# Windowed attention with a gated projection behind it: the same 1256 tasks written down in another order

## The chip, the core and the metric

The kernel runs on one core of a Trainium2 chip. The metric is the time of one execution on the device in microseconds (us). The engines of the core run at the same time, each through its own list of instructions in the order in which the program wrote them: TensorE (PE in the profile; its weight loads are PEld) multiplies into PSUM, VectorE (DVE) and ScalarE (ACT) read PSUM and do everything elementwise, GpSimd (POOL) is nearly unused, and SyncE (SP) issues DMAs. An instruction that waits holds up all that is behind it on its engine.

## The reference

There are 8 batches, 8 heads, 512 local and 32 global positions, head size 64. Local queries see the 32 global keys and the local keys at most 32 positions away; global queries see all 544 keys. The heads are put side by side (544 rows of 512 for each batch, the global ones ahead) and go through a gated projection with a causal convolution of 5 taps:

```python
s_ll = np.where(np.abs(pos[:, None] - pos[None, :]) <= 32, scale * q_l @ k_l.T, -1e9)
out_l = softmax(concat([scale * q_l @ k_g.T, s_ll])) @ concat([v_g, v_l])
out_g = softmax(scale * q_g @ k_all.T) @ v_all
x = concat([out_g, out_l]) as (batch, 544 positions, 512)
gate = sigmoid(sum_k conv_w[k] * x shifted by 4 - k positions)
return (gate * (x @ w_val)) @ w_out
```

## The kernel before, in words

The work is cut into 1256 named tasks. Each is a small Python function that issues a few instructions. The string `ORDER` (from line 60) lists all of them by name; the last loop of the kernel walks through the list and calls each function, under a manual schedule, so the list fixes the order of the instructions on every engine. It was written by a program that plans from costs of the tasks; the program is not part of the kernel. A name may carry two marks. `:ACT`, `:DVE` or `:SP` says which engine does it (a copy, a norm, a store), and `@46` in which of the 8 PSUM banks its result lies (here banks 4 and 6; a task that takes two neighbouring banks names the first). The dictionary `BY` holds the engines, `HOME` the banks.

There are 32 units u (a batch's pair of heads, 4 to a batch) and 16 pairs of units w. The tasks, with the lines of the profile that their instructions have:
- `iq` loads the keys and queries of a unit (592 KB), `ig` its values for the global queries, `iv` the local values of a pair (640 KB), `wi0` to `wi7` the quarters of the two weight matrices. All go through SyncE's queue at line 247 (`transfer`), where also most stores are issued (line 629).
- `s` computes the scores of a unit (lines 385 and 391, 72 matmul records), `mx` takes the row maximum (lines 396 and 398), `exp` the exponentials with their sums in two halves (line 406), `den` and `rec` the reciprocal (411, 415), `norm` multiplies a half by it (421 on ScalarE, as four instructions, or 423 on VectorE, as one), `t` transposes 32x32 blocks (429), `av` multiplies by the values (440, 160 records a pair), `xc` copies the result out of PSUM, `halo` fetches the four positions ahead of it.
- `gs`, `gmax`, `gexp`, `gt`, `gtc`, `gav`, `gden`, `grec`, `gnorm`, `gx`, `gxc` do the same for the global queries of a batch (lines 314 to 367; `gs` 32 records, `gt` 5, `gav` 80).
- `tap` and `conv` are the five taps (230 or 232, and 494), `pc` the same as a product with diagonal matrices for the first two units (510), `sig` the sigmoid (517), `xh` and `xl` split x into two parts of less precision (236 or 238, and 489).
- `g1.b.e.t` is a step of x @ w_val for batch b, output block e, input block t: three products of 128x512 (531). `gv` multiplies by the gate (538), `gh` and `gl` split again, `g2.b.r.e` is a step of the second product (555), `ob` copies a row block of 256 KB out of PSUM, `st` stores it. `.g.` in place of a batch is the part for the global positions of all batches; it comes last, and its second row block is done in two halves (`g2.g.1.0`, `g2.g.1.1`).
- `w0` to `w7` turn the 64-bit weights into two 32-bit parts (lines 204 to 214, 236, 283); `z` multiplies zeros to keep TensorE busy.

Three things decide what a place in the list means. Tiles come from rings of 1 to 6 buffers (`RINGS`: 4 for `qk`, 2 for `v`, 4 for `vg`, 2 for `ob`), so a task waits until the last reader of its buffer is done. A PSUM bank must be read out before the next task whose home it is writes it. And a load is held back until the last matmul that the list has ahead of it is done:

```python
ins = nc.sync.dma_start(out, in_).ins
if last_pe:
    tc.add_manual_dep(ins, last_pe[0].name, after, reason="a load's place in the line")
```

Of the kernel before, what the change touches and what calls it, by code (L numbers as in the profile page):

```python
# [65 lines left out]
w1.high:ACT w1.low gden0 t2 pc1.1 mx7 exp4.1 w2.s0:DVE pc1.2 exp5.0 xh0:ACT w3.s1 grec0 w3.s2 exp5.1 pc1.3 w2.s1 exp7.0
pc1.4 conv1.3:ACT w3.s3 wi4 den5 w2.s2 gnorm0 av1@24 ig5 exp7.1 wi7 pc0.0@0 ig7 den4 w3.s4 rec4 w2.s3 wi5 xc3:ACT iv2
rec5 ig6 norm4.1:ACT xc2:ACT gx0@1 den7 gs1@46 w2.s4 s6@2 norm4.0:ACT gxc0:DVE xh1:ACT tap3:ACT pc0.1 xl0 gmax1 iq8
tap2:ACT t4 gexp1.1 norm5.1:ACT xl1 halo1:ACT mx6 iq9 conv3.0 w2.high:DVE pc0.2 pc0.3 iq11 pc0.4 gexp1.0 fix1 g1.0.0.0@1
w3.high:ACT conv0.3:ACT exp6.0 g1.0.0.3 w3.low norm5.0:DVE g1.0.0.1 gt1.0@4 rec7 ig4 conv3.1 gt1.1@6 conv2.0 gtc1.0:ACT  # L70
g1.0.3.3@0 t5 iv3 exp6.1 conv2.1 iq10 fix0 s8@4 gtc1.1:ACT den6 g1.0.3.2 g1.0.0.2 gav1@6 g1.0.3.1 s9@2 norm7.0:ACT
w5.s0:ACT conv3.2 conv2.2 conv3.3 norm7.1:DVE sig0 gden1 conv2.3 w2.low g1.0.2.0@7 mx8 g1.0.2.1 sig1 g1.0.3.0 w5.s1
grec1 g1.0.2.2 w4.s0:ACT rec6 g1.0.2.3 mx9 gnorm1 gx1@6 exp8.0 gv.0.3 t7 gxc1:ACT w5.s2 exp8.1 exp9.0 g1.0.1.2@0
g1.0.1.3 w4.s1 g1.0.1.1 gv.0.2 w5.s3 g1.0.1.0 av2@46 gv.0.0 norm6.0:DVE norm6.1:ACT exp9.1 w4.s2 xc4:ACT gv.0.1 xc5:ACT
t6 ig10 gs2@02 iv5 w5.s4 w4.s3 w5.high:ACT gh.0.0:ACT ig11 gmax2 w5.low halo2:DVE den8 tap5:ACT ig9 gexp2.0 w4.s4 av3@46
iq12 ig8 gt2.0@0 gexp2.1 gt2.1@2 xc6:ACT gl.0.0 den9 s11@4 xc7:ACT w4.high:ACT s10@6 tap6:DVE gtc2.0:ACT w4.low
w6.s0:ACT w7.s0:ACT mx11 w6.s1 iv4 w6.s2 w7.s1 g2.0.0.0@0 g2.0.2.0@1 w7.s2 w6.s3 gtc2.1:ACT w7.s3 exp11.0 w7.s4 w6.s4
gh.0.1:ACT iq13 rec8 exp11.1 g2.0.1.0@2 g2.0.2.1 w6.high:DVE norm8.1:ACT w7.high:ACT g2.0.0.1 xh3:ACT g2.0.1.1
g2.0.3.0@3 iq14 gl.0.1 w6.low gav2@4 iq15 gden2 w7.low rec9 xl3 norm8.0:ACT g2.0.3.1 tap4:ACT g2.0.0.2 conv5.0 g2.0.0.3
t8 den11 g2.0.1.2 ob.0.0:ACT g2.0.3.2 g2.0.3.3 conv5.1 norm9.1:ACT halo3:DVE mx10 tap7:ACT g2.0.2.2 conv4.0 xh2:ACT  # L80
grec2 g2.0.2.3 ob.0.2:ACT g1.1.2.2@5 g2.0.1.3 xl2 g1.1.2.3 norm9.0:ACT gnorm2 exp10.0 s12@0 st.0.0:SP g1.1.1.0@4
st.0.2:SP ob.0.1:ACT t9 mx12 exp10.1 conv6.0 ob.0.3:ACT g1.1.2.0 g1.1.1.3 exp12.0 ig12 gx2@2 conv4.1 g1.1.1.1 conv6.1
rec11 den10 conv5.2 g1.1.3.2@3 st.0.3:SP gxc2:ACT conv7.0 g1.1.3.1 rec10 exp12.1 g1.1.0.0@2 conv6.2 conv5.3 conv4.2
g1.1.3.3 conv7.1 norm11.1:ACT av4@06 norm11.0:DVE g1.1.3.0 conv4.3 norm10.0:ACT g1.1.0.3 g1.1.2.1 norm10.1:ACT g1.1.0.1
g1.1.1.2 xc8:ACT conv7.2 st.0.1:SP t10 xc9:ACT conv7.3 g1.1.0.2 t11 conv6.3 halo4:ACT sig2 ig14 xh4:ACT gv.1.1 den12
gv.1.0 sig3 gv.1.2 av5@06 s13@4 gh.1.0:ACT xc10:ACT gv.1.3 gh.1.1:ACT gl.1.0 xc11:ACT gs3@02 rec12 mx13 gl.1.1
g2.1.2.0@6 g2.1.3.0@7 gmax3 tap8:ACT exp13.0 tap9:DVE conv8.0 xl4 g2.1.3.1 g2.1.2.1 iq16 ig15 exp13.1 g2.1.2.2 conv8.1
g2.1.3.2 g2.1.2.3 g2.1.3.3 xh5:ACT s14@4 gexp3.1 iq17 gexp3.0 xl5 ob.1.3:ACT s15@0 mx14 g2.1.1.0@7 st.1.3:SP tap10:ACT
g2.1.1.1 mx15 tap11:ACT ig13 halo5:DVE ob.1.2:ACT g2.1.1.2 exp14.0 g2.1.1.3 norm12.1:DVE exp14.1 den13 conv8.2 iv6
ob.1.1:ACT conv11.0 rec13 norm12.0:DVE conv10.0 g1.2.0.0@6 gt3.0@2 gt3.1@4 iq18 g1.2.1.1@7 g1.2.0.2 gtc3.0:ACT g1.2.0.3  # L90
gtc3.1:ACT gav3@4 g1.2.0.1 g1.2.1.3 g1.2.2.1@5 conv9.0 ig18 den14 norm13.1:ACT g1.2.1.0 t12 ig17 iv7 iq19 conv9.1
st.1.1:ACT exp15.0 conv8.3 conv10.1 conv9.2 gden3 norm13.0:ACT rec14 g1.2.2.3 t13 conv9.3 conv10.2 grec3 exp15.1
conv11.1 sig4 av6@02 norm14.0:ACT g1.2.1.2 den15 gnorm3 conv11.2 rec15 norm14.1:DVE g2.1.0.0@4 xc13:ACT g2.1.0.1 gv.2.0
st.1.2:SP conv10.3 xc12:ACT g1.2.2.0 gx3@6 tap12:ACT conv11.3 norm15.0:ACT gs4@02 gv.2.1 gxc3:ACT t14 s17@6 g2.1.0.2
gmax4 sig5 gexp4.1 mx17 gexp4.0 norm15.1:DVE g1.2.2.2 exp17.0 exp17.1 g2.1.0.3 tap13:DVE halo6:ACT g1.2.3.3@2 ig16 s16@0
ob.1.0:DVE g1.2.3.0 t15 xh6:DVE gt4.0@3 mx16 gh.2.0:DVE gtc4.0:ACT gv.2.2 gt4.1@6 gtc4.1:ACT den17 g1.2.3.2 g1.2.3.1
exp16.0 ig19 rec17 gv.2.3 conv12.0 gl.2.0 av7@36 exp16.1 s18@0 xc14:ACT iq20 s19@2 g2.2.0.0@4 g2.2.3.0@5 den16 xl6
g2.2.0.1 mx18 st.1.0:ACT gh.2.1:DVE norm17.0:ACT norm17.1:ACT iv8 xc15:ACT iq21 g2.2.3.1 exp18.0 gav4@6 rec16 gl.2.1
norm16.0:ACT t17 norm16.1:ACT iq22 exp18.1 g2.2.0.2 iq23 iv9 g2.2.1.0@7 ig23 halo7:DVE g2.2.0.3 conv12.1 xh7:DVE mx19
conv12.2 xl7 conv13.0 ob.2.0:ACT exp19.0 g2.2.3.2 s20@0 den18 g1.3.1.3@4 ig21 rec18 tap15:DVE gden4 exp19.1 norm18.1:ACT  # L100
# [5 lines left out]
g1.3.3.3@2 g1.3.3.1 g1.3.3.2 xh9:ACT halo9:DVE g1.3.2.1 g1.3.3.0 mx21 iq25 ig20 exp21.0 conv17.0 xl9 g1.3.2.3 tap19:DVE
gl.3.0 g1.3.2.0 exp21.1 gmax5 gexp5.0 st.2.2:SP gv.3.2 g2.3.0.0@0 gexp5.1 gv.3.3 conv19.0 g1.4.3.3@1 g1.4.3.0 gt5.0@2
gt5.1@4 g2.3.1.0@6 tap18:ACT g2.3.2.0@7 conv18.0 gtc5.0:ACT conv18.1 rec20 s22@2 gh.3.1:ACT gtc5.1:ACT den21 g2.3.2.1
conv19.1 rec21 conv18.2 gl.3.1 g1.4.3.1 mx22 norm21.1:ACT norm21.0:ACT norm20.1:ACT gav5@4 exp22.0 conv16.0 st.2.1:SP
t21 g2.3.0.1 g2.3.1.1 iv10 norm20.0:ACT conv19.2 g1.4.3.2 g2.3.2.2 conv17.1 gden5 g2.3.1.2 g2.3.0.2 grec5 g2.3.1.3 t20  # L110
exp22.1 den22 rec22 conv16.1 gnorm5 g2.3.2.3 g2.3.0.3 conv19.3 conv17.2 conv18.3 conv17.3 ob.3.1:ACT ob.3.2:ACT
norm22.0:ACT conv16.2 conv16.3 iq24 av10@24 sig8 sig9 gx5@7 st.3.1:SP g1.4.2.1@6 xc21:DVE g1.4.2.0 tap21:DVE ob.3.0:ACT
s23@4 gv.4.3 s24@0 mx23 xc20:ACT s25@2 gxc5:DVE g1.4.0.3@7 iq26 g1.4.0.1 g1.4.0.2 st.3.2:SP mx24 norm22.1:DVE mx25
tap20:ACT iv11 t22 g1.4.2.3 g1.4.2.2 g1.4.0.0 exp23.0 gv.4.0 exp23.1 exp25.0 exp24.0 exp24.1 den23 g1.4.1.2@4 halo10:DVE
rec23 iq27 g1.4.1.0 exp25.1 conv20.0 g2.3.3.0@7 g1.4.1.1 st.3.0:ACT g1.4.1.3 xh10:ACT norm23.0:DVE g2.3.3.1 g2.3.3.2
# [632 lines left out]
```

## Time and profile before

| what | us |
|---|---|
| runs of the kernel: median (lowest to highest) | 372.14 (370.38 to 375.02) |
| the profiled execution: its time | 370.21 |
| the profiled execution: span from first to last instruction | 368.4 |
| TensorE busy | 329.8 |
| VectorE busy | 310.5 |
| ScalarE busy | 266.9 |

The profile is of one execution. Between its span and its time lie 1.8 us that no instruction of the program shows. In a row of the timeline or of the waits, "issue" as the end of a wait means that the engine waited for no semaphore, queue or engine that the profile shows. A matmul's record is longer than the pitch at which matmuls follow each other, so a row of many is read by its whole length.

### The profile page before, as it was taken

Reading aid. Unit: us, or ns where it says so; the run is one execution under the profiler, and the core shown is the slowest. Engines: PE = TensorE matmul, PEld = TensorE weight load, DVE = VectorE, ACT = ScalarE, POOL = GpSimd, SP = SyncE. Lnnn points to the kernel's source line nnn. Section 1 sums busy time; section 2 is a strip of 40 time slices with the busy share of each in tenths; the row PEclk is TensorE's granted clock in tenths of the full one; section 3 lists DMA queues with packets and bytes.
Section 4 is the critical chain, followed back from the end, with each engine's and each line's share of the span. In section 5 each row is a group of like instructions: output and inputs, shape, how many; then the busy total and the mean of one; then the engine's idle time right before and its main releaser. Section 6 shows DMA issues by size and latency. Waiting matters only on the chain.

```text
span 368.4 us, 15320 instructions
## 1 busy us (share of the span) xinstructions
PE 329.8 (90%) x6736; PEld 257.4 (70%) x6736; DVE 310.5 (84%) x559; ACT 266.9 (72%) x855; POOL 1.0 (0%) x8
## 2 busy tenths in 40 slices
...
GB/s 284 377 389 74 132 357 240 2 282 147 189 95 40 97 234 252 63 104 200 369 12 4 161 87 100 264 121 269 169 73 202 75 69 91 30 2 30 86 59 114
DMA packets 19603, 54.76 MB, mean 149 GB/s; under 512 B 2128, under 2 KB 4560, under 8 KB 19536
## 3 DMA queue, kind: packets, MB, share of 16 engines
...
q8 instruction: 53, 0.87, 1.0%
...
## 4 chain that ended last, share of the span: by engine, by line
PE 63%; DMA 12%; DVE 12%; issue 6%; ACT 4%; SPq 1%; ACTq 0%; DVEq 0%
PE psum L531 19%; PE psum L555 18%; PE psum L440 9%; PE psum L385 8%; DMA qk<-in_qk_dram 5%; DVE gate L494 4%; DMA wraw<-in_w_val_dram 3%; PE psum L314 2%; PE psum L347 2%; DMA vg<-in_vgw_dram 2%; PE psum L331 2%; PE psum L510 2%; DMA craw<-in_convT_dram 1%; DVE pts L429 1%; DVE mx L396 1%
## 5 line engine op out<-in xcount | busy, mean ns | idle before, releaser
L406 ACT ACTIVATE pm<-psum,mx 128x128 f32<-128x128 f32 x256 | 90.5, 391 | 12.3 <-DVE mx L398 9.0
L494 DVE SCALAR_TENSOR_TENSOR gate<-xc,cw,gate 128x512 f32<-128x512 f32 x120 | 85.3, 741 | 0.6 <-ACT gate L230 0.2
L406 ACT ACTIVATION_READ_ACCUMULATOR pm<-psum,mx 128x1 f32 x256 | 59.1, 231 | 0.0
L385 PE MATMUL psum<-qk 64*32 64x128 f32 x2048 | 41.7, 279 | 16.7 <-issue 9.5
L531 PE MATMUL psum<-xh,wvh 128*128 128x512 f32 x128 | 53.4, 417 | 0.6 <-ACT pg L325 0.6
L396 DVE TENSOR_REDUCE mx<-psum 128x8 f32<-128x1024 f32 x32 | 38.9, 1217 | 16.6 <-PE psum L391 16.1
L555 PE MATMUL psum<-woh,gh 128*128 128x512 f32 x128 | 52.3, 409 | 0.0
L555 PE MATMUL psum<-wol,gh 128*128 128x512 f32 x128 | 50.5, 395 | 0.0
L555 PE MATMUL psum<-woh,gl 128*128 128x512 f32 x128 | 50.4, 394 | 0.0
L531 PE MATMUL psum<-xl,wvh 128*128 128x512 f32 x128 | 50.3, 393 | 0.0
L531 PE MATMUL psum<-xh,wvl 128*128 128x512 f32 x128 | 50.3, 393 | 0.0
L421 ACT ACTIVATE pm<-pm,mx 128x128 f32<-128x128 f32 x148 | 46.8, 408 | 4.8 <-DVE mx L415 4.6
L385 PEld LDWEIGHTS psum<-qk 64*32 64x32 f32 x2048 | 32.3, 107 | 25.4 <-issue 13.6
L440 PEld LDWEIGHTS psum<-pts,v 32*64 32x64 f32 x2560 | 38.1, 134 | 15.8 <-issue 9.1
L440 PE MATMUL psum<-pts,v 32*64 32x96 f32 (+3 forms) x2560 | 43.5, 264 | 6.0 <-issue 5.3
L429 DVE STREAM_TRANSPOSE pts<-pm 128x1024 f32<-128x1024 f32 x32 | 39.6, 1238 | 0.1
L531 PEld LDWEIGHTS psum<-xh,wvh 128*128 128x128 f32 x128 | 24.1, 188 | 8.5 <-issue 1.6
L555 PEld LDWEIGHTS psum<-woh,gh 128*128 128x128 f32 x128 | 24.3, 190 | 7.2 <-issue 2.1
L555 PEld LDWEIGHTS psum<-woh,gl 128*128 128x128 f32 x128 | 24.3, 190 | 5.4
L531 PEld LDWEIGHTS psum<-xh,wvl 128*128 128x128 f32 x128 | 24.0, 188 | 5.6
L517 ACT ACTIVATE gate<-gate 128x1024 f32<-128x1024 f32 x16 | 16.8, 1058 | 14.8 <-DVE gate L494 14.8
L555 PEld LDWEIGHTS psum<-wol,gh 128*128 128x128 f32 x128 | 24.4, 190 | 4.4
(106 smaller groups left out, 478.2 us busy)
## 6 DMA issues: line engine op xcount, KB each, us to landing
...
```

Of the source, the lines that this page charges most:

```text
L314: on_pe(T.matmul(s[h][SG * c:SG * c + SG, part], qkt[rows, C * GQ:C * GQ + C], qkt[rows, at:at + GH], start=True, stop=True))
L331: on_pe(T.transpose(pt[:, a, :], pg[:, h, P * a:P * a + P], ident))
L385: on_pe(T.matmul(s[h][C * j:C * j + C, P * i:P * i + P], qkt[rows, C * m:C * m + C], keys, start=(i == 0), stop=False))
L396: V.tensor_reduce(out=mx[:, :8], in_=banks(f"s{u}", 2).rearrange("p h (i c) -> p (h i) c", i=R), axis=AX.X, op=ALU.max, negate=True)
L406: A.activation(out=pm[:, h, i, :], in_=st[u]["s"][h][:, P * i:P * i + P], func=AF.Exp, bias=mx[:, c:c + 1], scale=SCALE, accum_out=mx[:, 8 ...
L421: A.activation(out=p[:, i, :], in_=p[:, i, :], func=AF.Copy, scale=rec[:, i:i + 1])
L429: V.transpose(out=st[w, "pts"][:, :, R * k:R * k + R].rearrange("p h i a q -> p h (i a q)"), in_=st.pop(u)["pm"].rearrange("p h i c -> p h ...
L440: on_pe(T.matmul(x[j // 2][D * h:D * h + D, j % 2, C * first:C * (first + count)], vt[rows, slot, h, :], p, start=(slot == 0), stop=stop))
L494: V.scalar_tensor_tensor(out=acc, in0=st[w, "xc"][:, t, k:k + SL], scalar=cw[:, u % NDT, k:k + 1], in1=acc, op0=ALU.mult, op1=ALU.add)
L517: A.activation(out=g, in_=g, func=AF.Sigmoid)
L531: on_pe(T.matmul(bank(f"g1.{key}.{e}")[:, :n], w[:, e, t * P:t * P + P], x, start=(d == 1 and q == 0), stop=(d == NDT and q == 2)))
L555: on_pe(T.matmul(o, g, w, start=(first and q == 0), stop=(last and q == 2)))
```

## The change

Only the text of `ORDER` differs: 1256 names before and after, the same names, in another order. The functions, rings, buffers and constants are the same, and each task issues the same instructions, except where a mark changes:
- engines: `norm` on ScalarE 41 of 64 halves (before 37), `halo` 11 of 15 (4), `ob` on ScalarE 32 of 35 (27, counting the two halves of the last block), `tap` 18 of 30 (20), `gtc` 16 of 16 (15), `gxc` 6 of 8 (5), `xh` 12 of 16 (13), the weights' first steps 2 of 8 (4) and their first copies 7 of 8 (6); the rest of each on VectorE. 28 of the 32 marked stores through SyncE (21) and 4 through ScalarE (11).
- banks: most `@` marks.

The diff, cut to the beginning, a piece of the middle and the end:

```diff
-iq0 iq1 iq2 iq3 wi0 iv0 wi1 iv1 wi2 wi3 cw z6.0@0 s0@0 gs0@24 dg0 mx0 gmax0 s1@6 dg1 exp0.0 exp0.1 w0.s0:DVE iq4 iq5
-s3@0 mx1 w0.s1 den0 gexp0.0 w1.s0:DVE exp1.0 rec0 w0.s2 gexp0.1 s2@2 gt0.0@4 exp1.1 z6.1@6 mx3 norm0.0:ACT ig0 w1.s1
-exp3.0 norm0.1:DVE mx2 iq6 iq7 den1 ig1 ig3 w1.s2 gtc0.0:ACT rec1 t0 exp3.1 norm1.1:DVE w0.s3 gt0.1@6 exp2.0 s4@4
-gtc0.1:ACT norm1.0:DVE w1.s3 ig2 w0.s4 t1 w0.high:ACT den3 exp2.1 mx4 av0@06 rec3 w0.low s5@2 norm3.1:DVE norm3.0:ACT
...
-g2.2.1.3 xh8:ACT gv.3.1 conv14.1 g1.3.0.2 den20 st.2.0:SP conv14.2 conv15.3 ob.2.1:ACT conv14.3 av9@04 tap16:ACT
-xc19:ACT halo8:ACT xc18:ACT st.2.3:SP gv.3.0 tap17:ACT xl8 gh.3.0:DVE g1.3.2.2@7 sig7 g2.2.2.3 s21@0 gs5@35 ob.2.2:DVE
...
-gv.g.1 g2.7.2.2 g2.7.1.3 ob.7.1:DVE gh.g.0:ACT g2.7.0.2 gv.g.3 g2.7.0.3 g2.7.2.3 gl.g.0 g2.g.1.0.0@5 g2.g.0.0@2
-ob.7.0:ACT gv.g.2 st.7.1:SP g2.g.0.1 gh.g.1:ACT gl.g.1 ob.7.2:DVE g2.g.1.0.2 g2.g.0.2 st.7.0:SP st.7.2:ACT ob.g.1.0:DVE
-g2.g.0.3 g2.g.1.1.0@3 ob.g.0:DVE g2.g.1.1.2 st.g.1.0 st.g.0 ob.g.1.1:ACT st.g.1.1
+iq0 iq1 iq2 iq3 wi0 iv0 wi1 iv1 wi2 wi3 cw z6.0@0 s1@0 mx1 dg0 s0@2 dg1 exp1.0 mx0 s3@4 mx3 z6.1@6 w0.s0:DVE exp1.1 den1
+gs0@06 w0.s1 rec1 w0.s2 gmax0 norm1.1:DVE ig2 iq4 exp0.0 exp3.0 exp0.1 w0.s3 iq5 norm1.0:ACT s2@2 den0 w1.s0:DVE gexp0.0
+gt0.0@0 rec0 w0.s4 w0.high:ACT norm0.1:ACT t1 w0.low gtc0.0:ACT gexp0.1 ig3 exp3.1 norm0.0:DVE w1.s1 mx2 t0 gt0.1@0
+w1.s2 w2.s0:DVE exp2.0 gtc0.1:ACT den3 w2.s1 rec3 w2.s2 w1.s3 w2.s3 norm3.1:DVE av0@46 exp2.1 den2 ig0 ig1 wi5 w2.s4
+norm3.0:ACT xc0:ACT s5@0 w1.s4 xc1:ACT rec2 halo0 pc0.0@6 pc0.1 w2.high:ACT w1.high:ACT mx5 s4@2 w1.low iq7 norm2.1:ACT
...
+sig1 s8@0 norm7.0:ACT xc5:ACT gh.0.0:ACT gav1@4 t6 ig11 w4.low iq11 mx8 g1.0.3.2 gl.0.0 g1.0.2.1 exp8.0 gden1 w7.s0:DVE
+grec1 exp8.1 ig8 w7.s1 s9@2 gv.0.3 gnorm1 norm7.1:ACT mx9 ig9 gv.0.2 gs2@04 tap5:ACT gmax2 g2.0.3.0@6 t7 w6.s1 exp9.0
...
+exp20.1 t18 gv.3.3 g1.3.2.0@2 mx21 g1.3.2.1 den20 halo8:ACT exp21.0 tap17:DVE g2.2.2.3 exp21.1 gh.3.0:DVE av9@63 gl.3.0
+tap16:DVE g1.3.2.2 g1.3.2.3 xc19:ACT gs5@03 xc18:ACT rec20 conv16.0 norm20.1:DVE den21 gv.3.2 gmax5 iv10 xh8:ACT
...
+g2.g.0.0@7 ob.7.1:DVE g2.g.1.0.0@6 gh.g.1:ACT g2.g.0.1 st.7.1:ACT gl.g.1 g2.g.1.0.2 ob.g.1.0:ACT g2.g.0.2 st.g.1.0
+g2.g.0.3 g2.g.1.1.0@6 g2.g.1.1.2 ob.g.0:ACT st.g.0 ob.g.1.1:ACT st.g.1.1
```

## Rows read from the trace of the kernel before

**Rows 1.** The page: its parts on engines (busy us, instructions) and on DMA queues

```profile
PE 329.8 (90%) x6736; PEld 257.4 (70%) x6736; DVE 310.5 (84%) x559; ACT 266.9 (72%) x855; POOL 1.0 (0%) x8
...
q8 instruction: 53, 0.87, 1.0%
```

**Rows 2.** Waits of TensorE, 0 to 100 us: waiting, ended by, total us, times, longest

```profile
PE psum L385 <- DMA qk<-in_qk_dram: 5.1, 5, 2.3
PE psum L385 <- issue: 4.8, 3, 2.8
PE psum L347 <- issue: 2.1, 2, 1.1
PE psum L314 <- issue: 1.3, 1, 1.3
PE psum L314 <- DMA qk<-in_qk_dram: 0.8, 1, 0.8
```

**Rows 3.** Waits of TensorE, 100 us to the end

```profile
PE psum L440 <- issue: 5.3, 6, 1.4
PE psum L385 <- issue: 4.8, 3, 2.3
PE psum L347 <- DMA vg<-in_vgw_dram: 2.5, 1, 2.5
PE psum L314 <- issue: 2.4, 2, 1.3
PE psum L385 <- DMA qk<-in_qk_dram: 1.4, 1, 1.4
PE psum L531 <- ACT pg L325: 0.6, 1, 0.6
```

**Rows 4.** Timeline of TensorE: start us, length us, line, what, count [idle before]

```profile
25.82 4.11 PE L440 MATMUL psum<-pts,v 32*64 32x256 f32 x160 [0.56 <-DVE mx L411]
...
31.40 0.74 PE L385 MATMUL psum<-qk 64*32 64x128 f32 x35 [0.89 <-issue]
...
34.81 1.22 PE L347 MATMUL psum<-vg,pgt 128*32 128x65 f32 x70 [1.13 <-issue]
...
40.45 2.44 PE L440 MATMUL psum<-pts,v 32*64 32x256 f32 x160
```

**Rows 5.** The chain that ended last, in order of time: start us, us, what

```profile
79.70 2.79 issue
...
92.33 5.68 PE psum L555 x24
...
208.80 1.09 PE psum L385 x64
...
243.61 2.28 issue
...
250.85 8.02 DMA vg<-in_vgw_dram
```

**Rows 6.** Windows: stretch, its us, busy us of each engine, clock, DMA share, GB/s

```profile
0.00:100.00 100.00, 83.53 (x2010) 60.36 (x2010) 81.87 (x169) 82.08 (x284) 1.04 (x8) 0.95 0.63 227
100.00:290.00 190.00, 172.96 (x3992) 136.40 (x3998) 166.94 (x283) 155.60 (x503) 0.00 (x0) 1.00 0.42 142
```

**Rows 7.** Instructions by line, ScalarE: busy us, mean ns | idle before, ended by

```profile
L421 ACT ACTIVATE pm<-pm,mx 128x128 f32<-128x128 f32 x148 | 46.8, 408 | 4.8 <-DVE mx L415 4.6
...
L236 ACT COPY ob<-psum 128x512 f32<-128x512 f32 x26 | 15.3, 589 | 16.3 <-PE psum L555 14.9 <-DMA out_dram<-ob 1.1
...
L517 ACT ACT_TABLE_LOAD x7 | 9.0, 1283 | 0.9 <-DVE gate L476 0.8
```

**Rows 8.** Timeline of VectorE, from 11 to 13 us

```profile
11.21 1.36 DVE L321 TENSOR_REDUCE gm<-psum 128x1 f32<-128x544 f32 x2 [1.52 <-PE psum L314]
...
12.68 0.42 DVE L206 TENSOR_SCALAR wa<-wraw 128x512 int32<-128x512 int32 x1
```

**Rows 9.** Timeline of ScalarE, the last copy

```profile
364.07 0.37 ACT L236 COPY obg<-psum 128x256 f32<-128x256 f32 x1 [5.03 <-DMA out_dram<-obg]
```

More of the change, by code (lines that the diff above doesn't have):

```diff
@@ L66 @@
[L66 to L100, printed above, removed]
@@ L106 @@
[L106 to L115, printed above, removed]
@@ L116 @@
-conv21.0 gv.4.2 g2.3.3.3 gv.4.1 ob.3.3:ACT gs6@02 norm23.1:DVE den24 t23 st.3.3:SP ig24 den25 gh.4.0:ACT gh.4.1:DVE iv12
-av11@46 gmax6 gexp6.0 gexp6.1 gl.4.1 xc22:ACT xc23:ACT gt6.0@0 gl.4.0 tap22:ACT gt6.1@2 s26@4 rec24 rec25 s27@6
-gtc6.0:DVE mx26 g2.4.3.0@0 norm25.0:DVE halo11:DVE iq29 iq30 norm25.1:ACT ig27 gtc6.1:ACT tap23:ACT g2.4.3.1 xh11:DVE
-g2.4.3.2 ig26 ig25 g2.4.2.0@1 xl10 exp26.0 xl11 g2.4.3.3 t25 g2.4.2.1 g2.4.1.0@2 conv21.1 conv20.1 conv21.2 norm24.0:ACT
-ob.4.3:ACT norm24.1:ACT mx27 st.4.3:ACT g1.5.3.3@0 exp26.1 g2.4.2.2 conv22.0 exp27.0 g2.4.1.1 g2.4.1.2 den26 conv20.2
@@ new lines @@
+exp16.0 conv10.2 exp16.1 t14 conv11.1 exp17.0 ig18 g1.2.2.1 g1.2.3.1 st.1.2:SP iq19 g1.2.3.0 ig19 exp17.1 g1.2.2.3
+g1.2.0.3 tap12:ACT conv10.3 g1.2.0.2 conv11.2 ig16 conv11.3 sig5 g2.1.0.3 av7@03 xc15:ACT xc14:ACT xh6:DVE g1.2.2.2
+g1.2.0.1 den16 xl6 gv.2.3 gv.2.2 gv.2.0 xh7:ACT g1.3.1.0@4 gs4@02 xl7 gmax4 tap15:ACT halo6:ACT s18@6 ob.1.0:ACT
+gh.2.0:ACT iv8 gexp4.1 mx18 iq21 iq20 rec16 st.1.0:SP gexp4.0 den17 ig17 g1.3.0.0@5 g1.3.1.1 gh.2.1:DVE gl.2.0 g1.3.1.2
+g1.3.1.3 g1.3.0.1 halo7:ACT gt4.0@0 g1.3.0.3 norm16.1:ACT gtc4.0:ACT gl.2.1 conv13.0 conv12.0 tap14:DVE g2.2.3.0@2
@@ new lines @@
+exp18.0 conv12.1 exp18.1 s19@0 g2.2.0.0@3 g2.2.0.1 norm16.0:ACT rec17 mx19 norm17.1:ACT conv13.1 iq23 den18 t16 gt4.1@6
+gtc4.1:ACT g2.2.0.2 g2.2.3.1 conv13.2 g2.2.3.2 conv12.2 norm17.0:ACT g2.2.3.3 exp19.0 ob.2.3:ACT t17 gav4@6 g2.2.0.3
+conv13.3 conv15.0 conv12.3 exp19.1 conv15.1 ob.2.0:ACT conv14.0 gden4 g2.2.1.0@7 rec18 sig6 g2.2.1.1 conv14.1 grec4
+den19 g1.3.0.2 g2.2.1.2 st.2.3:SP gnorm4 av8@02 ig20 norm18.1:ACT conv15.2 rec19 xc16:ACT iv9 xc17:ACT g1.3.3.1@6
+g2.2.1.3 g1.3.3.3 conv14.2 gx4@2 norm19.0:DVE ig22 ob.2.1:ACT s21@0 st.2.1:SP norm19.1:ACT gv.3.1 conv15.3 s20@3 gv.3.0
@@ new lines @@
+g2.2.2.0@5 conv14.3 mx20 gxc4:ACT iv11 g1.3.3.2 norm18.0:ACT t19 sig7 exp20.0 g2.2.2.1 iq22 st.2.0:SP g2.2.2.2 g1.3.3.0
+exp20.1 t18 gv.3.3 g1.3.2.0@2 mx21 g1.3.2.1 den20 halo8:ACT exp21.0 tap17:DVE g2.2.2.3 exp21.1 gh.3.0:DVE av9@63 gl.3.0
+tap16:DVE g1.3.2.2 g1.3.2.3 xc19:ACT gs5@03 xc18:ACT rec20 conv16.0 norm20.1:DVE den21 gv.3.2 gmax5 iv10 xh8:ACT
+gh.3.1:ACT s23@6 ob.2.2:ACT g2.3.3.0@2 g2.3.2.0@5 gl.3.1 st.2.2:SP g2.3.2.1 ig21 gexp5.1 iq26 mx23 rec21 gexp5.0 gt5.0@0
+g2.3.2.2 ig23 halo9:ACT conv16.1 norm20.0:ACT t20 tap19:DVE norm21.0:DVE g2.3.3.1 xh9:ACT iq25 g2.3.2.3 g2.3.3.2 s22@3
@@ new lines @@
+exp23.0 gtc5.0:ACT conv17.0 ob.3.2:ACT mx22 norm21.1:ACT g2.3.3.3 xl9 g2.3.0.0@5 conv17.1 exp23.1 gt5.1@0 gtc5.1:ACT
+iq24 g2.3.0.1 g2.3.0.2 ob.3.3:ACT t21 gav5@0 g2.3.0.3 exp22.0 st.3.2:SP conv17.2 st.3.3:SP xl8 conv16.2 iq27 den23
+exp22.1 g1.4.0.2@1 den22 g2.3.1.0@2 g1.4.0.1 av10@36 g2.3.1.1 gden5 rec22 tap18:ACT grec5 rec23 ob.3.0:ACT conv18.0
+g1.4.0.0 norm23.1:DVE gnorm5 conv17.3 norm23.0:ACT conv16.3 g2.3.1.2 conv19.0 norm22.1:DVE norm22.0:ACT xc20:ACT s24@3
+st.3.0:SP ig27 ig25 conv18.1 xc21:ACT t22 s25@5 mx24 g1.4.0.3 sig8 mx25 g1.4.1.2@7 g1.4.1.1 gv.4.0 t23 exp24.0 conv19.1
```

86 lines of the change are left out of this document (58 added, 28 removed).

## The prediction, made before the changed kernel ran

> **What bounds the kernel now.** I began with the page: TensorE is busy for 329.8 of 368.4 us, VectorE for 310.5, ScalarE for 266.9 [rows 1]. TensorE sets the time, and the first thing to read is why it ever stands still. Its waits, read once up to 100 us and once after, answer that. Up to 100 us 4.8 + 2.1 + 1.3 = 8.2 us are ended by "issue" (nothing that the profile shows) and 5.1 + 0.8 = 5.9 us by a load that landed [rows 2]; after it 5.3 + 4.8 + 2.4 = 12.5 us and 2.5 + 1.4 = 3.9 us [rows 3]. The largest wait on another engine after 100 us is 0.6 us. An order that has ScalarE or VectorE done earlier would gain little; one that removes part of the 20.7 and the 9.8 would.
>
> **What "issue" is.** Queue 8, kind instruction, moved 53 packets with 0.87 MB [rows 1], 16.4 KB each. TensorE has 6736 matmuls and as many weight loads, and 13472 / 53 = 254: one packet carries about 127 matmuls with their loads; I call that a line. In TensorE's timeline two stops follow each other at 31.40 and 34.81 us [rows 4], with 127 matmuls from one to the other (eight rows of S, mask and value products stand between). So a stop comes at the end of a line, and a line with little work still takes 34.81 - 31.40 = 3.4 us. The work in it is far less: 64 products of S take 1.09 us [rows 5], 160 of av 2.44 us [rows 4], so 128 of either are 2.0 to 2.2 us. 24 products of a projection take 5.68 us [rows 5]: a line of those lasts 30 us and never stops. A stop is then 3.4 us less the work of its line, and that work depends on which tasks the order puts side by side.
>
> [...]
>
> **Part 1, short lines.** I walked both orders, adding matmuls as the code issues them (s 72, av 160, gs 32, gav 80, gt 5, a g1 or g2 task 3), cut them every 127.6 through the stop at matmul 733 (34.81 us), and priced each line with the rows above. Before: 19 lines under 3.4 us, together 20.4 us short, against 20.7 measured; so I trust the sum (single lines agree less well: first rival). After: 13 lines, 9.4 us short. The change sets projection triples between the runs of av and s; only av0, av8, av11, av12 and av15 still hold a whole line. Lines 16 to 50 begin at about 100 us:
> - Lines 16 to 50: 12.4 us short before (12.5 measured), 6.0 after. TensorE is busy 173.0 of 190 us there, VectorE 166.9, ScalarE 155.6 [rows 6], so TensorE's time is the stretch's: **-6.4**.
> - Lines 1 to 15: 7.9 before, 3.4 after; this goes into part 3.
>
> **Part 2, loads after 100 us.** A load is issued when the TensorE task ahead of it in the order is done and its buffer is free, so its lead is the TensorE work between that place and its first reader. The 3.9 us stood at iq20 and iq21 (lead 4.7 to 8 us) and at ig25, ig26 (6.2 us; two qk and three vg loads were issued together, and one took 8.02 us [rows 5]). In the new order the shortest leads here are 6.5 (ig24, ig26), 6.6 (ig23), 7.1 (ig14) and 7.5 us (iq22). I leave 0.6 us for them: **-3.3**, between 0 (a crowded load takes 8.0 again) and -3.9. Seven more stores go through SP (28, before 21), and a load behind a store waits for that store's copy. The loads of the shortest leads have at most one such store ahead, so I count 0; if that fails, it eats the 3.3.
>
> **Part 3, the head.** TensorE could gain 4.5 us from lines and some of the 5.9 from loads (iq4 and iq5 were awaited before s4; now av0 stands between them and their reader). But VectorE and ScalarE are busy 82 of these 100 us each [rows 6] and start late. The new order does max 1, 0 and 3, then w0.s0, which could run at 12.68 us [rows 8], and then gmax0. That needs gs0, which now stands behind s3 and behind the first line's stop: VectorE waits some 2.7 us there where it waited 1.52 [rows 8]. From then to t0, on which av0 waits, I count 9 us, so av0 starts near 25.5, as before (25.82), and probably again at the half clock that made it 4.11 instead of 2.44 us [rows 4]. By a quarter of TensorE's work VectorE has been given as much work as before (84 against 85 us) and ScalarE 1.5 us more. Of their 18 idle us, 8 lie before 16 us; of the other 10 perhaps half were waits on TensorE's stops and come back: 5, less 1.0 lost at the start: **-4.0**, with 0 and -8 as ends.
>
> **Part 4, work that changes engine.** Four norm halves go to ScalarE, 4 x 4 x 0.408 = 6.5 us; five result copies too, at about 0.59 (three of them shorter), 2.7 us [rows 7]; the small ones (halo, tap, gtc, gxc, weights) give -0.6. VectorE loses about 6 us. Sigmoid and exp alternate 19 times instead of 13, so six more table loads at 1.283: 7.7 us [rows 7]. ScalarE gets 16.3 us more. From 100 to 290 us it has 34 us idle, so most is covered; but part of that cover was there because TensorE stood still. With fewer stops a PSUM bank must be read sooner after it is written. One place I can see is gs2, which needs the bank that exp8.1 reads, behind a table load, while TensorE has some 3 us of work. I charge **+3.0**: no row shows such a wait, the nearest (0.6 us, on ScalarE [rows 3]) is small; the ends are 0 and 16.3.
>
> **Part 5, the end.** The last copy waits until 364.07 for the store of the first half [rows 9]; it does so again, after the same last products: 0.
>
> Sum: -6.4 - 3.3 - 4.0 + 3.0 = -10.7. The profiled execution took 370.2 (span 368.4 and 1.8 around it), so 359.5. It was a quick one, the median of the runs being 372.14, 1.9 more: 361.4. I say **361**.
>
> **Rivals.**
> 1. *The fetch is late, not only slow.* The stops from 79.70 and 243.61 us took 2.79 and 2.28 us [rows 5], where those lines held 2.9 us of work each and my bound gives 0.5. The new order lifts lines from 2 us to just above the floor: 12 of its lines hold 3.4 to 4.5 us, 5 of the old. If each of the 12 stops 0.5 us, the 6.4 shrinks to 0.4: 367. For it: the load queues are busy 42% of the middle stretch [rows 6]. Against it: the sum over all lines met the measured one. Chance 0.22.
> [...]
> 3. *ScalarE takes over.* All of its 16.3 us lands ahead of bank reads that TensorE awaits: 372.14 - 13.7 + 16.3 = 375, slower. It decides from 13.7 us of such waits on. For it: six table loads stand ahead of an exp, and exps free the banks of s. Against it: 0.6 us of such waits now. Chance 0.06.
> 4. *The head gives 8 and nothing is lost to ScalarE*: 372.14 - 17.7 = 354. Chance 0.10.
>
> **How the numbers follow.** Forecast 0.54, rivals 0.22, 0.08, 0.06, 0.10. Two per cent, about what a measurement of this kernel can tell from no change, is 7.4 us: faster is under 364.7, slower over 379.6. The forecast's own range is 357 to 365.5, a tenth of it over 364.7: faster 0.48 + 0.10 + 0.02 (of rival 1) = 0.60; slower, half of rival 3, 0.03; within, 0.37. The range takes in rival 1 and the better part of rival 4: 354 to 369.
>
> **What would show it.** Right: TensorE's waits on "issue" fall to 9 to 11 us and those on loads to 5, none over 2 after 100 us; stops remain in av8, av11, av12 and av15; ScalarE shows 19 table loads after the first and some 283 us busy. Rival 1: stops of 0.5 to 2 us in lines that hold 3.4 to 4.5 us. [...] Rival 3: TensorE's waits on ScalarE over 13. The head is wrong if av0 starts before 24 or after 28 us.

## The result, and the profile after

| | before | after |
|---|---|---|
| median of the runs, us (lowest to highest) | 371.46 (370.38 to 375.02) | 358.61 (357.83 to 361.46) |
| ratio, 95% interval | | 0.965 (0.957 to 0.974) |
| the profiled execution: its time, us | 370.21 | 357.83 |
| its span, us | 368.4 | 354.9 |

The changed kernel is faster. Run twice more beside other kernels it came to 0.954 (0.949 to 0.959) and 0.958 (0.956 to 0.961) of the kernel before, so a single comparison of it is good to about half a per cent. I forecast 361.0 us with a range of 354 to 369: the time is right. Of the steps under it, the first 100 us came out on the other side, and the part behind them gave half as much again as foreseen.

The page of the changed kernel, engines (busy us, share, instructions) and DMA queues, against [rows 1]:

```profile
PE 328.3 (93%) x6736; PEld 255.5 (72%) x6736; DVE 304.5 (86%) x545; ACT 278.6 (78%) x887; POOL 1.0 (0%) x8
...
q8 instruction: 52, 0.85, 1.0%
```

TensorE does the same work in 13.5 us less span, with one packet fewer on queue 8 (one such packet is what I call a fetch from here on). The waits of TensorE in the changed kernel, first from 0 to 100 us (waiting, ended by, total us, times, longest), against [rows 2]:

```profile
PE psum L331 <- ACT pg L325: 5.2, 2, 3.7
PE psum L391 <- issue: 3.3, 1, 3.3
PE psum L440 <- issue: 3.3, 1, 3.3
PE psum L347 <- issue: 1.8, 1, 1.8
PE psum L385 <- DMA qk<-in_qk_dram: 1.3, 2, 0.7
PE psum L314 <- ACT pm L406: 1.3, 2, 1.0
PE psum L385 <- ACT xc L236: 1.2, 1, 1.2
```

and from 100 us to the end, all of them, against [rows 3]:

```profile
PE psum L440 <- issue: 2.1, 2, 1.2
PE psum L331 <- ACT pg L325: 0.6, 1, 0.6
PE psum L331 <- ACT xc L236: 0.3, 1, 0.3
```

The second list carries the gain. After 100 us the stops on "issue" fall from 12.5 to 2.1 us and the waits on loads (2.5 + 1.4, and 0.3 of a second kind) from 4.2 to nothing: 14.6 us. Waits on ScalarE grow by 0.3. The first list shows none of it: "issue" 8.2 before and 8.4 now; loads fall from 5.9 to 1.3, and ScalarE takes their place, 8.2 us with the smaller rows, 0.9 before.

The windows of the changed kernel (stretch, its us, busy us of PE, PEld, DVE, ACT, POOL, clock, DMA share, GB/s), against [rows 6]:

```profile
0.00:100.00 100.00, 80.71 (x1927) 57.39 (x1928) 79.78 (x162) 81.75 (x295) 1.05 (x8) 0.91 0.61 211
100.00:290.00 190.00, 187.27 (x4290) 148.19 (x4289) 176.86 (x300) 171.67 (x556) 0.00 (x0) 1.00 0.48 157
```

From 100 to 290 us TensorE goes from 173.0 to 187.3 us busy out of 190. In the first 100 us it loses 2.8 busy us and the mean clock falls from 0.95 to 0.91. The two orders do different tasks there, so I priced the matmuls done by 100 us as the prediction does: 73.2 us of TensorE's own work before, 69.4 after (70.9 in a second execution). By this estimate the changed kernel is 2.3 to 3.8 us behind at 100 us.

### The profile page after: what moved, and what is told of

Same layout as the page of the kernel before. It is cut to its first block, busy times and chain, and to the rows that moved or that the text cites. A ratio compares the mean times of both kernels' runs of the same rounds, so it can differ in the third digit from the quotient of the medians.

```text
span 354.9 us, 15327 instructions
## 1 busy us (share of the span) xinstructions
PE 328.3 (93%) x6736; PEld 255.5 (72%) x6736; DVE 304.5 (86%) x545; ACT 278.6 (78%) x887; POOL 1.0 (0%) x8
## 4 chain that ended last, share of the span: by engine, by line
PE 72%; DVE 15%; ACT 5%; issue 4%; DMA 2%; SPq 0%; ACTq 0%; DVEq 0%
PE psum L555 23%; PE psum L531 22%; PE psum L440 10%; PE psum L385 7%; DVE gate L494 3%; PE psum L347 3%; DMA qk<-in_qk_dram 2%; DVE pts L429 2%; DVE mx L396 2%; PE psum L331 2%; PE psum L314 2%; PE psum L510 2%; DVE gm L321 1%; ACT pm L406 1%; DVE xl L489 1%
## 5 line engine op out<-in xcount | busy, mean ns | idle before, releaser
L406 ACT ACTIVATION_READ_ACCUMULATOR pm<-psum,mx 128x1 f32 x256 | 60.5, 236 | 0.0
L555 PE MATMUL psum<-woh,gh 128*128 128x512 f32 x128 | 53.3, 416 | 0.0
L421 ACT ACTIVATE pm<-pm,mx 128x128 f32<-128x128 f32 x164 | 52.4, 413 | 0.4 <-DVE mx L415 0.4
L440 PEld LDWEIGHTS psum<-pts,v 32*64 32x64 f32 x2560 | 38.0, 135 | 15.1 <-issue 8.2
L440 PE MATMUL psum<-pts,v 32*64 32x96 f32 (+3 forms) x2560 | 42.8, 266 | 6.5 <-issue 5.4
L385 PE MATMUL psum<-qk 64*32 64x128 f32 x2048 | 38.1, 278 | 2.5 <-DMA qk<-in_qk_dram 1.3
L385 PEld LDWEIGHTS psum<-qk 64*32 64x32 f32 x2048 | 31.1, 107 | 11.8 <-issue 6.1
L538 DVE TENSOR_TENSOR gv<-psum,gate 128x512 f32<-128x512 f32 x32 | 21.8, 685 | 7.8 <-PE psum L531 5.3
L236 ACT COPY ob<-psum 128x512 f32<-128x512 f32 x29 | 17.2, 601 | 14.2 <-PE psum L555 10.9
```

What stands on the lines that cost most here:

```text
L236: A.copy(out, in_)
L385: on_pe(T.matmul(s[h][C * j:C * j + C, P * i:P * i + P], qkt[rows, C * m:C * m + C], keys, start=(i == 0), stop=False))
L406: A.activation(out=pm[:, h, i, :], in_=st[u]["s"][h][:, P * i:P * i + P], func=AF.Exp, bias=mx[:, c:c + 1], scale=SCALE, accum_out=mx[:, 8 ...
L421: A.activation(out=p[:, i, :], in_=p[:, i, :], func=AF.Copy, scale=rec[:, i:i + 1])
L440: on_pe(T.matmul(x[j // 2][D * h:D * h + D, j % 2, C * first:C * (first + count)], vt[rows, slot, h, :], p, start=(slot == 0), stop=stop))
L538: V.tensor_tensor(out=box["gv", p][:, k], in0=bank(f"g1.{key}.{e}")[:, :n], in1=gates[w0 + p][:, k], op=ALU.mult)
```

## The experiments

**1. Do stops belong to lines?** Dummy products of 64 columns behind gt0.0 move every later line boundary against the tasks by 16 or by 64 matmuls; no task changes its place.

```diff
+            if name == "gt0.0":
+                for _ in range(16):        # 64 in the second kernel
+                    T.matmul(psum[:C, 1, 2 * P:2 * P + 2 * C], eye[:D], mask[:D, :2 * C], start=True, stop=True)
```

> The changed order with 16 small matmuls of constants put behind gt0.0, where TensorE has 3.7 us to wait; nothing of the result depends on them. They push every later line boundary back by 16 matmuls of the order's own, so other tasks share a line. Theory A (stops come at line boundaries, and the new order was fitted to where they lie): lines 19, 24, 32, 45 and 48 are now short without long products right before them, and stops after 100 us grow from 2.1 us to 6 to 9 us; the time grows by 3 to 6 us over the changed kernel (ratio to before 0.974 to 0.982). Theory B (stops belong to the small matmuls themselves): stops stay at 2 us and the time within 1 us (0.965). Theory C (3.4 us less the line's own work, as in the prediction, whatever comes before the line): 7.2 us of short lines against 6.0, so 1.2 us more.

> As the run before, with 64 of the small matmuls in place of 16: some 1 us of work in a gap of 3.7 us. It is the control for what the added matmuls cost themselves. Theory A: the boundaries fall again so that long products stand before every short line; stops after 100 us stay at 1 to 3 us, the time within 1.5 us of the changed kernel (ratio 0.962 to 0.970). Theory B: the same. If the added matmuls cost by themselves, this run is slower than the one with 16.

With 16: 363.15 us, 0.973 of before (0.967 to 0.978). With 64: 356.14, 0.955 (0.950 to 0.959), no slower than the changed kernel itself. The waits of TensorE after 100 us with 16 dummies (columns as above):

```profile
PE psum L440 <- issue: 5.3, 4, 1.6
PE psum L391 <- issue: 1.6, 1, 1.6
...
PE psum L531 <- issue: 0.3, 1, 0.3
```

7.2 us of stops where the changed kernel has 2.1, and 3.5 with 64 dummies. Sixteen tiny products cost 5 us or more (0.973 against the 0.954 and 0.958 of the changed kernel alone, measured at other times; 5.1 us of it are these stops) and 64 cost nothing: what counts is where the boundaries fall. Stops belong to lines.

**2. What hides a fetch?** In the changed kernel av8, av11, av12 and av15 each hold a whole line, done in 1.8 to 2.1 us, and show no stop where the prediction's bound asks for 1.4 each. Their boundaries stand 2, 4, 3 and 5 matmuls behind projection triples. The kernel before has the same kind of line with other distances (worked out from its trace: packets of queue 8, and TensorE's starts at the boundaries):

```
line's products   matmuls between the last    fetch begins, us from       stop at the
                  long products and boundary  TensorE's passing boundary  line's end, us
before av4        30                          +0.52                       1.40
before av10       22                          -0.15                       0.66
before av9        12 (9 long ones ahead)      +0.72                       1.16
before av13       14 (gs7 between)            +1.08                       1.27
before av15       10                          -0.31                       0.41
before av12       7                           -0.27                       none
after  av12       3                           -0.55                       none
after  av11       4                           -1.17                       none
after  av8        2                           -2.27                       none
after  av15       5                           -3.03                       none
```

So the fetch of the next line may begin before TensorE reaches the boundary. I read it so: TensorE's sequencer, whose waits for semaphores the profile records (PEldq), runs ahead while long products (0.23 us each) wait to be done. In the trace of before its wait in front of av4 is on record at 105.4 us, 1.7 us ahead of av4's first product. To test that on one line, six triples of the kernel before went from right behind av4 to right ahead of it, which leaves 12 matmuls of av4 ahead of the boundary in place of 30 and the 128 matmuls of the line what they were.

```diff
-av4@06 norm11.0:DVE g1.1.3.0 conv4.3 norm10.0:ACT g1.1.0.3 g1.1.2.1 norm10.1:ACT g1.1.0.1 g1.1.1.2 ... g1.1.0.2
+g1.1.3.0 g1.1.0.3 g1.1.2.1 g1.1.0.1 g1.1.1.2 g1.1.0.2 av4@06 norm11.0:DVE conv4.3 norm10.0:ACT norm10.1:ACT ...
```

> The order before, with six triples of the projection (g1.1.3.0, 0.3, 2.1, 0.1, 1.2, 0.2) moved from right behind av4 to right ahead of it. The line boundary in av4 stood 30 matmuls into it and stands 12 into it now; the 128 matmuls up to the next boundary are products of av4 as before, 1.95 us. Theory A (the sequencer runs ahead of TensorE while long products stand before a boundary, so that the fetch begins earlier): the stop at the end of that line, 1.4 us, falls to 0.6 or less. Theory B (the prediction's bound: 3.4 us less the line's work): it stays at 1.4. Both: the other stops unchanged within 0.3 us. The time changes by 1 us at most, too little to read by itself.

373.44 us, 1.001 (0.997 to 1.005). TensorE's timeline around av4 (start us, length us, line, what, count [idle before]), first before:

```profile
107.07 2.40 PE L440 MATMUL psum<-pts,v 32*64 32x256 f32 x157
110.87 0.33 PE L440 MATMUL psum<-pts,v 32*64 32x32 f32 x3 [1.40 <-issue]
```

then with the triples ahead:

```profile
110.69 0.39 PE L531 MATMUL psum<-xh,wvl 128*128 128x512 f32 x1
111.01 2.44 PE L440 MATMUL psum<-pts,v 32*64 32x256 f32 x160
114.10 2.13 PE L440 MATMUL psum<-pts,v 32*64 32x256 f32 x97 [0.66 <-ACT xc L236]
```

All 160 products of av4 run through. The fetch began 2.84 us before TensorE passed the boundary, not 0.52 after it (0.85 after it, with a stop of 1.47 us, in the trace of experiment 3, where av4 stands as before). Long products ahead of a boundary let the fetch begin early, and the fixed floor of the prediction falls. The time did not move: av5, which the triples no longer separate from av4, now waits 0.66 us for ScalarE, and the s behind it 1.8 us for VectorE. The other stops did not stay as they were, as I had expected: the next three (1.27, 0.44 and 1.12 us) are gone too, with waits on VectorE and on a load in the place of two of them, and the one near 246 us is 0.5 us shorter. All stops after 100 us add up to 8.5 us here, 12.5 before.

**3. Loads alone.** The kernel before with four loads moved up, all matmuls in place:

```diff
-s16@0 ... iq20 ... iq21 ... iq27 ... ig26 ig25
+s16@0 iq20 iq21 ... iq27 ig26 ig25 ...
```

> The order before, with four loads moved up alone: iq20 and iq21 right behind s16, ig25 and ig26 right behind iq27; nothing else differs and no matmul changes its place. Theory A (part 2: the waits on loads after 100 us are lost time of TensorE): the waits on loads after 100 us fall from 4 us to under 1 and the time by 3 to 4 us, to 0.990 of the kernel before. Theory B (the wait is only moved: what stands behind is late for another reason): waits on loads gone, the time within 1 us. Theory C (loads moved up stand in the way of the fetches): the stops on issue after 100 us grow, from 12.5 to 14 or more, and the time is the same. If late fetches come from loads in flight, the stop of 2.3 us at 246 us changes too, since two of the five loads around it are now elsewhere: to 1 or less.

371.39 us, 0.992 (0.988 to 0.997): about 2.9 us of 373. The waits of TensorE after 100 us:

```profile
PE psum L440 <- issue: 6.5, 6, 1.5
PE psum L385 <- issue: 4.5, 4, 1.9
PE psum L314 <- DMA qk<-in_qk_dram: 2.9, 1, 2.9
PE psum L314 <- issue: 1.8, 1, 1.8
```

The waits at iq20, iq21 and at ig25, ig26 are gone, and part of them came back as time. One of 2.9 us on a load that was not moved (for gs4) stands here; it was 0.3 in the trace of before and 2.6 in the experiment on av4, so it seems to vary between executions. Stops stayed at 12.8 us: loads moved up do not get in the way of fetches here. The stop of 2.3 us near 246 us measured 1.6, but 1.7 in the experiment on av4, where no load was moved, so that expectation has no support.

**4. The head.** Edits of the changed kernel: without the zeros z6.1 (below); with the loads iq7 and iq6 right behind gt0.1; both; and, in two versions, the beginning rewritten with gs0 ahead of s3 and without the zeros.

```diff
-s3@4 mx3 z6.1@6 w0.s0:DVE
+s3@4 mx3 w0.s0:DVE
```

> The changed order without z6.1, six products of zeros that stand between s3 and gs0 and whose result nobody reads (left out). In the profile of the changed kernel they take 2.9 us at the half clock, between the first stop and gs0, on the chain that leads to av0 at 28.97 us. Theory A (the head is a chain over gs0, gmax0, gexp0, and the zeros are on it): gs0 starts 2.9 us earlier, av0 1 to 2.9 us earlier, the whole 1 to 2.5 us less (ratio 0.958 to 0.963). [...]

> The changed order with the loads iq7 and iq6 (issued at 37.4 and 42.8 us) right behind gt0.1, at about 28 us, when few loads run. Theory A (a fetch that is asked for while loads run starts late: the one that ended the stop of 3.28 us at 48.85 started 5.0 us after its boundary was reached, 1.1 us being the usual): the stops at 41.43 and 48.85 (1.75 and 3.28 us) fall to 2 us or less together, with perhaps one new stop of up to 2 us in av0, which now runs beside the loads; the time falls by 1 to 3 us (ratio 0.957 to 0.963). Rival (these stops are lines with little work, loads or not): they stay, the time within 0.5 us.

> The changed order without the six zero products z6.1, and with the loads iq7 and iq6 right behind gt0.1. Theory A (the head of the changed kernel is held by two separate things: TensorE's own queue delays gs0 and by it av0 by 3 us, and the fetch under the loads stops it for 3.3 and 1.75 us at 41 and 49 us): both gains add, 4 + 2.6, so 352 us, with av0 near 25.8 and no stop over 1.5 us before 60 us. Theory B (VectorE and ScalarE set the head, and whatever TensorE saves is waited for later on them): no better than the run without zeros, 354 to 355 us, with TensorE's waits on ScalarE or VectorE up by 2 to 3 us between 40 and 100 us. Theory C (the boundaries, shifted by six matmuls, matter more): stops after 100 us differ by over 3 us from the 2.7 of the run without zeros.

> The changed kernel itself, once more, so that the edits to it can be compared within one session. Theory and rivals expect the same: about 358.6 us, 0.965 of the kernel before, stops of TensorE after 100 us of 2 us together and about 8 us of waits on ScalarE in the first 100 us. If it comes out under 357, part of what the runs without zeros and with earlier loads seemed to gain was the chip's drift between sessions.

Alone they measured 354.66 us, 0.950 (0.947 to 0.953), and 355.97, 0.950 (0.942 to 0.957); both together, at another time, 356.77, 0.959 (0.953 to 0.964), beside the changed kernel's own 356.31, 0.954 (0.949 to 0.959). That is under the 357 that I had set as the sign of a drift between the sessions, and what the two seemed to gain alone is not there together. The zeros may be worth 1 or 2 us; the runs don't settle it.

> The changed order with its first microseconds mended: gs0 and gmax0 ahead of s3 (as before; for that gs0 takes banks 4 to 7, s3 banks 0 and 1, gt0.0 bank 4), no zeros z6.1, and the two exponentials gexp0.0 and gexp0.1 directly behind exp1.1 and norm0.1. Theory A (part 3 failed because gs0 stands behind s3, the first line's stop and the zeros, so that VectorE and ScalarE get the global scores late): the global maximum starts before 13 us (19.93 in the changed kernel), av0 near 26 (28.97), TensorE's waits on ScalarE at gt0.0 and gt0.1 fall from 5.2 to under 2 us, and the time to 353 to 354 us. Theory B (VectorE's and ScalarE's own work up to av0 sets its start, whatever stands first): av0 at 27 or later and the time that of the changed kernel. In both the stops after 100 us are those of the run without zeros, 2 to 5 us.

357.13 us, 0.958 (0.953 to 0.962). In this kernel s3 stands ahead of exp1.1 in the list and takes the banks that exp1.1 reads, so that half of unit 1's softmax is made from unit 3's scores and exp1.1 waits for s3; its time decides nothing. Put right:

```diff
-s0@2 dg1 exp1.0 mx0 s3@4 mx3 z6.1@6 w0.s0:DVE exp1.1 den1 gs0@06 w0.s1 rec1 w0.s2 gmax0 ... gexp0.0 gt0.0@0
+s0@2 dg1 exp1.0 mx0 gs0@46 gmax0 w0.s0:DVE exp1.1 gexp0.0 s3@0 den1 w0.s1 rec1 mx3 w0.s2 ... gt0.0@4
```

> As the run before it, with s3 behind exp1.1 and gexp0.0, so that it no longer overwrites the scores that exp1.1 reads and exp1.1 no longer waits for it. Theory A (gs0 behind s3, the first line's stop and the zeros is what made the head late): global maximum before 13 us, TensorE's waits on ScalarE before av0 under 2 us together, av0 near 25 to 26, time 353 to 354 us, 0.948 to 0.950 of the kernel before. Theory B (VectorE's and ScalarE's own work up to av0 sets its start): the maximum is early, but av0 starts at 27 or later behind the transposes t0 and t1, and the time is within 1.5 us of the changed kernel, 0.954 to 0.962.

354.75 us, 0.953 (0.949 to 0.957). VectorE's timeline, the global maximum (19.93 us in the changed kernel):

```profile
10.85 1.36 DVE L321 TENSOR_REDUCE gm<-psum 128x1 f32<-128x544 f32 x2 [0.15 <-PE psum L314]
```

TensorE's waits of this kernel, 0 to 100 us:

```profile
PE psum L385 <- ACT pm L406: 5.5, 3, 4.2
PE psum L440 <- issue: 2.9, 2, 2.7
PE psum L385 <- ACT xc L236: 1.2, 1, 1.2
PE psum L314 <- ACT pm L406: 1.0, 1, 1.0
PE psum L331 <- ACT pm L406: 0.9, 1, 0.9
```

The maximum is 9 us earlier, av0 starts at 25.69 (28.97), the stop in the first line is 0.6 us (3.3) and the waits at gt0.0 and gt0.1 fall from 5.2 to 1.1. Where the 28.97 came from is seen in TensorE's and then VectorE's timeline of the changed kernel, with the first stop, the zeros and av0, and with the maxima of s3 and of gs0:

```profile
14.68 0.40 PE L391 MATMUL psum<-consts 64*32 64x256 bf16 x3 [3.28 <-issue]
15.01 2.93 PE L626 MATMUL psum<-zr 128*128 128x512 f32 x6
...
28.97 3.91 PE L440 MATMUL psum<-pts,v 32*64 32x256 f32 x160 [0.80 <-DVE pts L429]
15.12 1.22 DVE L396 TENSOR_REDUCE mx<-psum 128x8 f32<-128x1024 f32 x1 [3.91 <-PE psum L391]
...
19.93 1.36 DVE L321 TENSOR_REDUCE gm<-psum 128x1 f32<-128x544 f32 x2 [2.13 <-PE psum L314]
```

and of the kernel with 64 dummies, which has the same beginning:

```profile
13.84 1.66 PE L626 MATMUL psum<-zr 128*128 128x512 f32 x6
...
25.72 3.81 PE L440 MATMUL psum<-pts,v 32*64 32x256 f32 x160 [0.56 <-DVE pts L429]
16.68 1.35 DVE L321 TENSOR_REDUCE gm<-psum 128x1 f32<-128x544 f32 x2
```

From the global maximum to av0 it is 9.0 us in both, and also with 16 dummies, without the zeros, with the early loads, with both, and in the control of experiment 5. The maximum is late because VectorE waits 3.91 us for s3, which the first stop holds up, and 2.13 us for gs0 behind the zeros. The zeros took 2.93 us in the first trace, at a granted clock of 0.5, and 1.66 us in the second, at 1.0, where the wait for gs0 is missing. So with the zeros av0 started anywhere between 25.72 and 28.97 us; without them alone it started at 25.83, with both small edits at 26.76. One trace of each kernel does not show what the zeros are worth.

With gs0 first av0 comes near 25.7 as theory A has it, but hardly earlier than the best of these, and the time lies between the two theories. TensorE now waits 4.2 us at s2 for ScalarE to read out exp0.1, and its waits on ScalarE in the head are 9.1 us in all, no less than the 8.2 of the changed kernel. Part of it comes from the new order itself: ScalarE waits 1.68 us for the maximum of the delayed s3 before it gets to exp0.1. Against the 0.954 and 0.958 of the changed kernel this order is 0 to 0.5% better, with intervals that overlap; no version of the study is shown to beat it.

**5. The engine marks.** The changed order and banks, with all 97 marks that differ put back to the engines of before:

```diff
-... norm1.0:ACT ... norm0.1:ACT ... w2.high:ACT ... w3.s0:ACT ... halo2:ACT ... ob.1.0:ACT ...
+... norm1.0:DVE ... norm0.1:DVE ... w2.high:DVE ... w3.s0:DVE ... halo2:DVE ... ob.1.0:DVE ...
```

> The changed order and banks, but every task on the engine that it had before (97 marks put back: norms, taps, halos, copies, stores). Theory A (part 4 of the prediction: ScalarE's added work costs TensorE 3 us): with it gone ScalarE has some 8 to 10 us less work (the table loads stay, they come from the order) and the time falls by 2 to 3 us against the changed kernel. Theory B (after 100 us TensorE sets the time and the engines have slack, so the marks are worth nothing there): within 1.5 us of the changed kernel, waits of TensorE after 100 us on VectorE or ScalarE under 2 us. Theory C (the order was fitted to its marks, and putting back the old ones makes VectorE late at single places): over 2 us slower, with new waits of TensorE on VectorE of that size.

> The changed kernel once more, beside the two others: 356 to 359 us, 0.954 to 0.965 of the kernel before, as in the two sessions before this one. The stops of TensorE at the boundaries in gav0, av1 and in lines 24 and 34, which were 1.75, 3.28, 1.16 and 0.99 us in one execution and 0.33, 3.00, 2.55 and 0.95 in another, differ again by up to 1.5 us if the fetch competes with the loads, and agree within 0.3 if its time is fixed by the program.

375.98 us, 1.011 (1.008 to 1.014), against 356.66, 0.958 (0.956 to 0.961), for the changed kernel beside it: 19 us slower, and slower than before the change. The longest of TensorE's waits after 100 us:

```profile
PE psum L440 <- ACT pm L406: 2.4, 2, 1.9
PE psum L531 <- DVE ob L238: 2.3, 1, 2.3
PE psum L440 <- issue: 2.3, 1, 2.3
PE psum L331 <- ACT pg L325: 2.0, 2, 1.2
PE psum L440 <- DVE pts L429: 1.8, 1, 1.8
PE psum L555 <- DVE gvg L538: 1.0, 1, 1.0
```

Waits on VectorE and ScalarE, 0.9 us in the changed kernel, add up to 12 here, in a dozen places. VectorE has 6.9 us more work and ScalarE 6.6 us less than in the changed kernel, which reads as tasks on the wrong engine at single places, not as one engine that is full. A wait can also have a tail. TensorE's timeline behind the one of 2.27 us:

```profile
174.04 0.50 PE L531 MATMUL psum<-xh,wvh 128*128 128x512 f32 x1 [2.27 <-DVE ob L238]
...
176.16 0.63 PE L531 MATMUL psum<-xl,wvh 128*128 128x512 f32 x1
176.58 0.63 PE L531 MATMUL psum<-xh,wvl 128*128 128x512 f32 x1
...
178.72 0.40 PE L531 MATMUL psum<-xl,wvh 128*128 128x512 f32 x1
178.95 0.39 PE L531 MATMUL psum<-xh,wvl 128*128 128x512 f32 x1
```

From 175.3 to 178.7 us the granted clock is 0.5, and a product comes every 0.43 us where it came every 0.23. In the kernel before the clock fell to 0.5 in the same way behind the stop of 2.79 us (from 83.8 to 87.2 us), and stayed at 1.0 behind the one of 2.28 us (243.61 us). Which of the 97 marks carry the 19 us was not tried.

In the control's trace the stops after 100 us are 1.17 and 1.20 us, against 1.16 and 0.99 in the first profile; in the head 2.68 against 3.28, and the one of 1.75 in gav0 is missing. Where boundaries lie is the program's; how long some stops are is in part the execution's.

## Why the prediction was right, point by point

- **What bounds the kernel, and the line.** Right. TensorE's stops on "issue" were the largest thing to win, and they go by lines of 128 matmuls (experiment 1). In the changed kernel crossing a boundary costs up to 3.3 us where small products follow each other, and nothing among long ones.
- **Part 1, -6.4: mis-sized, measured -10.4.** The step that failed is the fixed floor, "a stop is then 3.4 us less the work of its line". It holds only where the fetch begins about 1.1 us after TensorE has passed the boundary. In experiment 2 the fetch of one and the same 128 products began 0.5 us behind the boundary or 2.8 us ahead of it, by what stood in front. So "stops remain in av8, av11, av12 and av15" was wrong: there were none, and the 6.0 us that the bound left after 100 us were 2.1. The sign "fall to 9 to 11 us" for all of "issue" came true by luck: it is 10.5, but 8.4 of it in the head, where 3.4 were foreseen. The change gained by putting long products ahead of boundaries, not only by lengthening lines. That the bound met the sum of the kernel before (20.4 against 20.7) came of errors that cancelled: it asks for 1.4 us in av12, where there was no stop, and for 0.5 at 79.70 and at 243.61 us, where 2.79 and 2.28 were measured. That single lines agreed less well, as the prediction says, was the sign to follow.
- **Part 2, -3.3: right, measured -4.2.** Experiment 3 gets -2.9 (-1.3 to -4.5) from the loads alone. The leads of 6.5 to 7.5 us were enough.
- **Part 3, -4.0: wrong, measured +2.3 to +3.8.** Two steps failed. TensorE was to gain 4.5 us from lines, and "issue" took 8.4 us of the head where it had taken 8.2. And "av0 starts near 25.5": it started at 28.97 (28.01 in the control of experiment 5), outside the 24 to 28 that I allowed, though at 25.72 with the 64 dummies. The 9 us from the global maximum on were right. Its start was not: I counted 2.7 us of VectorE's wait for gs0 and left out the six zeros, and VectorE waited 3.91 us for s3 behind the first line's stop and 2.13 us for gs0 behind the zeros. gt0.0 and gt0.1 then wait 5.2 us for the global exponentials. The 5.9 us of loads did go, to 1.3, but ScalarE's 8.2 us of waits came in.
- **Part 4, +3.0: wrong as a cost after 100 us, and the marks were read the wrong way.** The 19 table loads behind the first came as counted [rows 7]. ScalarE's busy time grew by 11.7 us to 278.6, not by 16.3 to 283: 21.7 us more in the sum of its records, which overlap; the four instructions of a norm half last 1.3 us together, not 4 x 0.408. After 100 us TensorE waits 0.9 us for it; the wait that the prediction named, gs2's for the exponentials, is there, 1.3 us at 80.44 us in the head. I read the marks as work moved onto ScalarE and charged for it; put back alone they cost 19 us. An engine's total told nothing of that.
- **Part 5, 0: right in size.** From the last product's start to the end of the span 4.5 us, 4.8 before [rows 9]. But the last copy does not wait for the store again: it waits 0.89 us, for TensorE.
- **Rivals.** The first, that a fetch is late, is real but small: both stops left after 100 us follow a late fetch (next section), 2.1 us, not the 6 that it asked for; that loads make it late is not shown. The second, that stops belong to the small matmuls and not to lines, fell with experiment 1. The third needed 13.7 us of waits on ScalarE; there are 9.1. The fourth had its total nearly right (354 against 356 to 359), by other terms.

So the gain came from the two sources that I named, short lines and loads behind 100 us, but 361 came near by luck: part 1 was 4 us too small, part 4 charged 3 us that did not come up after 100 us, and the head was 6 to 8 us too good. The parts as measured, -10.4, -4.2, +0.3 for ScalarE after 100 us and the +2.3 to +3.8 of the head, add up to -12.0 to -10.5, and the span fell by 13.5: 1.5 to 3 us are not accounted for.
